# Differences of the blocks of x in the second phase: GpSimd in place of VectorE

## The chip, the cores and the metric

The kernel runs on one core of one Trainium2 chip. The metric is the device time of one execution in microseconds (us), from outside; three executions of the kernel before gave 1159.93, 1160.05 and 1161.06 us, median 1160.05. The engines in the profile are PE (TensorE matmuls), PEld (its weight loads), DVE (VectorE), ACT (ScalarE), POOL (GpSimd) and SP (SyncE, which issues all DMAs here).

## The reference

Linear attention over 8 batches and 8 heads, then a gated feed-forward layer on its output:

```python
def phi(x):
    proj = np.einsum('bhsd,df->bhsf', x, w_phi)
    proj = proj - np.max(np.abs(proj), axis=-1, keepdims=True)
    return np.concatenate([np.exp(proj), np.exp(-proj)], axis=-1)
q_p, k_p = (phi(q), phi(k))
kv = np.einsum('bhsf,bhsd->bhfd', k_p, v)
z = np.sum(k_p, axis=2)
num = np.einsum('bhsf,bhfd->bhsd', q_p, kv)
den = np.einsum('bhsf,bhf->bhs', q_p, z)[..., None] + 1e-06
attn = num / den                    # q, k, v: 8 x 8 x 576 x 64; w_phi: 64 x 128

x = attn.transpose(0, 2, 1, 3).reshape(4608, 512)
gate = 1.0 / (1.0 + np.exp(-(x @ w_gate)))      # 512 x 1536
val = x @ w_val                                 # 512 x 1536
out = gate * val @ w_out                        # 1536 x 512
```

## The kernel before

**Two phases.** The first phase (to about 610 us) makes the attention, writes its output x to DRAM in chunks of 512 tokens (`xscr`), and computes the part of the feed-forward layer that belongs to the first 512 of the 1536 hidden features (lines 914 and 971). The second phase does the other 1024 hidden features in two rounds of 512, each over 6 blocks of 768 tokens (`DC`): twelve passes of `pass_over`. Each pass adds its part of the output to what the rounds before left in DRAM.

**Precision by splitting.** A matmul in full float32 is replaced by three in the faster type float32r: each operand is split into a high part (a cast, on ScalarE) and a low part (the operand less its high part, a subtraction on VectorE), and high x high, high x low and low x high are summed.

**Blocks of x.** The products of the second phase are done on 2 x 2 blocks with seven products in place of eight, so that differences of the blocks of x are needed. `x_blocks` prepares them for one pass. It fetches four blocks of 128 x 768 (two of 128 features side by side, 384 tokens each) into `b11`, `tmp[0]` (block 12), `b22` and `b21`, makes four differences with `less` (the instruction is at line 1178), and splits seven blocks with `split`: a cast on ScalarE (line 1187) and a subtraction on VectorE (line 1191). The split of a fetched block is done in place: its low part overwrites the block, so it must wait until the differences that read the block are done. The differences are tmp[1] = tmp[0] - b11, tmp[2] = b22 - tmp[1], tmp[0] = b22 - tmp[0], and, once tmp[2] has been split, tmp[2] = b21 - tmp[2].

**A pass.** For each of two pairs of hidden blocks `group` runs seven products for the gate and seven for the value (line 1229: 6 matmuls of 128 x 384 each, into five PSUM banks named `bank`), and VectorE adds the products up (line 1242, one operand in PSUM, one in SBUF). `gated` applies the sigmoid on ScalarE, `valued` multiplies by the value (line 1280) and splits the result into its high (line 1284, ScalarE) and low part (line 1288, VectorE). Then six output tiles of 128 tokens are computed (line 1311: 12 matmuls of 128 x 512 each, 6 for each pair, into three PSUM banks named `gate`), and VectorE adds the earlier part from DRAM as it drains a bank (line 1139). The blocks of x of the next pass are fetched and made around the boundary between the products of one pass and its output tiles. In the first four passes VectorE also prepares weights for the second round (lines 796 to 867 and 1069 to 1094).

**What sets the order.** A planner (`Plan`) runs once on the host. Each step is given to it with an engine, a busy time, a lag, what it reads and writes and a rank; the planner simulates the engines, and from the steps that could start soonest takes the one with the lowest rank. The instructions are then written in the order of their planned starts. On the chip each engine works through its own queue in that order, and waits at an instruction until the semaphores of its inputs and of its output buffer are there.

Of the kernel before, what the change touches and what calls it, by code (L numbers as in the profile page):

```python
# [34 lines left out]
HT = 384  # L35
# [113 lines left out]
class Plan:  # L149


    SWITCH = 0.15
    NEAR = {"PE": 0.3, "DVE": 0.05, "ACT": 0.05, "SP": 0.0, "X": 0.0}
    SAME = {"PE": 0.0, "DVE": 0.12, "ACT": 0.13, "SP": 0.0, "X": 0.0}
    RATE = 0.26

    def __init__(self):
# [21 lines left out]
    def run(self):  # L179
        free = dict.fromkeys(self.NEAR, 0.0)  # L180
        ready = {e: [] for e in free}
# [31 lines left out]
        while left:  # L213
            best = None
            for e, cs in ready.items():
                ts = [(t, o) for o in cs if (t := start(o)) is not None]
                if not ts:
                    continue
                first = min(t for t, _ in ts) + self.NEAR[e]

# [32 lines left out]
            for n in o.then:  # L253
# [3 lines left out]
                else:  # L257
                    at = t + o.busy + self.SAME[o.eng]
                n.ready = max(n.ready, at)
# [8 lines left out]
def attention_moe(  # L268
# [9 lines left out]
    nc = tc.nc  # L278
    vec, act = nc.vector, nc.scalar
# [99 lines left out]
    plan = Plan()  # L379
# [4 lines left out]
    def dve(n, fn, reads, writes, rank, k=1.0, after=()):  # L384
        return plan.op("DVE", 0.07 + n / 960 / k, 0.16, fn, reads, writes, rank, after=after)

    def on_act(n, fn, reads, writes, rank, after=()):
        return plan.op("ACT", 0.08 + n / 1200, 0.17, fn, reads, writes, rank, after=after)

    def sp(size, fn, reads, writes, rank, after=()):  # L390
        return plan.op("SP", 0.06, size, fn, reads, writes, rank, after=after)
# [757 lines left out]
    def x_blocks(dc, r):  # L1149

        at_ = {n: (Buf([r_X], [P, 2, HT]), Buf([r_X], [P, 2, HT])) for n in XB}
        tmp = [Buf([r_tmp], [P, 2, HT]) for _ in range(3)]
        n_, since = [0.0], len(plan.ops)

        def rank():
            n_[0] += 0.1
            return r + n_[0]

        def fetch(x, K, h):
            t, e = dc * DC + h * HT, dc * DC + h * HT + HT  # L1160
            s = 0
            while t < e:
                c, o = divmod(t, CW)
                wd = min(CW - o, e - t)
                sp(
                    wd << 10,
                    lambda c=c, o=o, s=s, wd=wd: nc.sync.dma_start(
                        x().bitcast(F32)[:, :, s : s + wd],
                        xscr[c][:, 2 * K : 2 * K + 2, o : o + wd],
                    ),  # L1170
                    [xmark[c]], [x], rank(), prior[-1:],
                )
                t, s = t + wd, s + wd

        def less(o, a, b):
            dve(
                2 * HT,
                lambda: vec.tensor_tensor(  # L1178
                    o(), a().bitcast(F32), b().bitcast(F32), op=ALU.subtract
                ),  # L1180
                [x for x in (a, b) if x is not o], [o], rank(),
            )

        def split(n, src):
            xh, xl = at_[n]
            on_act(
                2 * HT, lambda: act.copy(xh(), src().bitcast(F32)), [src], [xh], rank()  # L1187
            )
            dve(
                2 * HT,  # L1190
                lambda: vec.tensor_tensor(
                    xl(), src().bitcast(F32), xh().bitcast(F32), op=ALU.subtract
                ),
                [src, xh] if src is not xl else [xh], [xl], rank(),
            )

        b11, b21, b22 = (at_[n][1] for n in ("11", "21", "22"))
        fetch(b11, 0, 0)
        fetch(tmp[0], 0, 1)
        fetch(b22, 1, 1)  # L1200
        fetch(b21, 1, 0)
        less(tmp[1], tmp[0], b11)
        split("11", b11)
        less(tmp[2], b22, tmp[1])
        split("T2", tmp[2])
        less(tmp[0], b22, tmp[0])
        split("T3", tmp[0])
        split("T1", tmp[1])
        less(tmp[2], b21, tmp[2])
        split("21", b21)  # L1210
        split("T4", tmp[2])
        split("22", b22)
        prior.append(plan.op("X", 0.0, 0.0, lambda: None, after=plan.ops[since:]))
        return at_
# [206 lines left out]
```

## Time and profile before

| what | us |
|---|---|
| median of three runs | 1160.05 |
| the profiled execution | 1160.85 |
| its span, first to last instruction | 1158.9 |
| TensorE busy | 1142.8 |
| VectorE busy | 933.3 |
| ScalarE busy | 583.0 |
| GpSimd busy (six instructions at the start) | 0.7 |

Times inside the program are counted from the start of the span. The profiled execution's own time is 1.95 us longer than its span. A line such as "L1178 DVE TENSOR_TENSOR more<-low,more x24" is a group: the line of the kernel, the engine, the operation, the tile written and the tiles read (`low`, `high`, `flat` and `more` are the four large SBUF areas in which the planner places its buffers, `bank` and `gate` are PSUM), and how often. In a timeline the two numbers ahead are the start and the length in us, and brackets behind name what ended the idle time in front of an instruction.

### The profile page before, as it was taken

What the parts mean: (1) busy time and instruction counts of PE and PEld (TensorE: products, weight loads), DVE (VectorE), ACT (ScalarE), POOL (GpSimd) and SP (SyncE); (2) the same over time, 40 slices, a digit from 0 to 9 for tenths busy, and PEclk for the clock granted to TensorE, in tenths of its full rate; (3) what the DMA queues carried; (4) which work ended last, traced back from release to release, by engine and by line L of the source; (5) the groups of instructions that cost most, each with busy time, mean ns of one, the idle gap of its engine ahead of it and who ended that gap; (6) DMA issues with size and microseconds to landing.
All of it is one profiled execution on the core that took longest, in us unless ns stands there. A gap on an engine that the chain in (4) does not pass through costs nothing.

```text
span 1158.9 us, 22323 instructions
## 1 busy us (share of the span) xinstructions
PE 1142.8 (99%) x8796; PEld 939.5 (81%) x8796; DVE 933.3 (81%) x1793; ACT 583.0 (50%) x1115; POOL 0.7 (0%) x6
## 2 busy tenths in 40 slices
PE   8999999999999999999999999999999999999998
PEld 6666566766676677678889999999999999999997
DVE  6999989888878878847897999988767757757764
ACT  6867776666656666635553444352332333323421
POOL 0000000000000000000000000000000000000000
PEclk9999999999999999999999999999999999999999
DMA  6764554344424443226526656545447433225122
GB/s 237 226 220 127 152 168 123 121 129 137 137 87 153 121 137 122 70 79 209 173 101 211 206 178 223 187 141 186 154 173 286 141 106 123 78 88 163 56 95 82
DMA packets 99441, 171.08 MB, mean 148 GB/s; under 512 B 18825, under 2 KB 43529, under 8 KB 99337
## 3 DMA queue, kind: packets, MB, share of 16 engines
q1 hardware_dynamic: 99336, 169.66, 45.7%
q8 instruction: 69, 1.13, 0.4%
q14 instruction: 36, 0.29, 0.1%
HBM read 120.06 MB, written 49.42 MB: 146 GB/s over the span
## 4 chain that ended last, share of the span: by engine, by line
PE 84%; DVE 7%; DMA 6%; ACT 2%; issue 1%; SPq 1%; DVEq 0%
PE bank L1229 30%; PE gate L1311 17%; PE gate L914 11%; PE gate L971 6%; PE bank L621 4%; PE bank L663 3%; PE bank L914 3%; DMA rb<-den 3%; PE bank L432 2%; PE bank L681 2%; DMA den<-dn 2%; PE bank L537 1%; DVE d L587 1%; PE bank L971 1%; PE bank L635 1%; PE bank L647 1%
## 5 line engine op out<-in xcount | busy, mean ns | idle before, releaser
L1229 PE MATMUL bank<-low,high 128*128 128x384 f32 x2016 | 351.8, 336 | 0.0
L1229 PEld LDWEIGHTS bank<-low,high 128*128 128x128 f32 x2016 | 349.8, 188 | 1.1
L1311 PE MATMUL gate<-low 128*128 128x512 f32 x864 | 198.4, 389 | 0.0
L1311 PEld LDWEIGHTS gate<-low 128*128 128x128 f32 x864 | 162.0, 188 | 33.2
L914 PE MATMUL gate<-low 128*128 128x512 f32 x696 | 165.7, 393 | 1.2 <-ACT flat L949 0.6
L914 PEld LDWEIGHTS gate<-low 128*128 128x128 f32 x696 | 128.6, 188 | 29.7 <-issue 1.2
L479 ACT ACTIVATE ek<-ek 128x512 f32<-128x512 f32 (+1 forms) x192 | 96.6, 526 | 27.3 <-DVE ek L467 25.9
L1242 DVE TENSOR_TENSOR more<-more,bank 128x384 f32<-128x384 f32 x111 | 61.1, 551 | 40.8 <-PE bank L1229 40.3
L971 PE MATMUL gate<-low 128*128 128x512 f32 x384 | 92.3, 394 | 0.0
L971 PEld LDWEIGHTS gate<-low 128*128 128x128 f32 x384 | 70.8, 188 | 15.1 <-issue 1.0
L621 PE MATMUL bank<-ek,vin 128*32 128x256 f32 x1240 | 74.5, 386 | 4.4 <-ACT d L545 3.8
L621 PEld LDWEIGHTS bank<-ek,vin 128*32 128x32 f32 x1240 | 37.8, 110 | 46.2 <-issue 11.0
L1139 DVE TENSOR_TENSOR flat<-gate,low 128x512 f32<-128x512 f32 x72 | 49.3, 685 | 23.3 <-PE gate L1311 11.7
L438 DVE TENSOR_REDUCE mk<-bank 128x4 f32<-128x512 f32 (+1 forms) x92 | 49.0, 552 | 21.3 <-PE bank L432 16.9
L1242 DVE TENSOR_TENSOR flat<-flat,bank 128x384 f32<-128x384 f32 x75 | 41.3, 551 | 29.3 <-PE bank L1229 29.1
L1187 ACT CAST low<-more 128x768 fp32r<-128x768 f32 x36 | 30.1, 836 | 61.1 <-DVE more L1178 60.8
L467 DVE TENSOR_TENSOR ek<-bank,mk 128x512 f32<-128x512 f32 (+1 forms) x92 | 48.2, 550 | 0.6 <-ACT d L550 0.2
L1267 ACT ACTIVATE more<-more 128x384 f32<-128x384 f32 x38 | 20.0, 525 | 57.1 <-DVE more L1242 56.9
L938 ACT CAST low<-flat 128x512 fp32r<-128x512 f32 x36 | 22.3, 620 | 51.5 <-DVE flat L963 44.9
L1284 ACT CAST low<-more 128x384 fp32r<-128x384 f32 x50 | 24.7, 513 | 46.6 <-DVE more L1280 46.6
L590 ACT ACTIVATE eq<-d 128x1152 f32<-128x1152 f32 x29 | 33.9, 1168 | 24.8 <-DVE d L587 24.4
L432 PE MATMUL bank<-wk,kin 64*128 64x128 f32 x496 | 38.7, 289 | 4.6 <-DMA kin<-k 4.3
(184 smaller groups left out, 1700.1 us busy)
## 6 DMA issues: line engine op xcount, KB each, us to landing
flat<-w_moe SPq DMA_DIRECT2D x36, 512.0 KB
low<-xs SPq DMA_DIRECT2D x46, 256.0 KB
kin<-k SPq DMA_DIRECT2D x32, 320.0 KB
qin<-q SPq DMA_DIRECT2D x32, 320.0 KB
vin<-v SPq DMA_DIRECT2D x32, 320.0 KB
ys<-flat SPq DMA_DIRECT2D x36, 256.0 KB
low<-ys SPq DMA_DIRECT2D x36, 256.0 KB
yt<-flat SPq DMA_DIRECT2D x36, 256.0 KB
```

Of the source, the lines that this page charges most:

```text
L432: nc.tensor.matmul(pk[hd]()[:, t, :], x()[head(hd), t * P : t * P + P], wk[head(hd), :], start=True, stop=True,)
L438: vec.tensor_reduce(mx, pk, axis=AX.X, op=ALU.max, apply_absolute_value=True)
L467: vec.tensor_tensor(ek[g]()[:, :, F:], src, mk[g]()[:, :ns].unsqueeze(2).broadcast_to([P, ns, F]), op=ALU.subtract,)
L479: lambda g=g, sg=sg: act.activation(ek[g]()[:, :, sg * F : sg * F + F], ek[g]()[:, :, F:], AF.Exp, scale=1.0 - 2.0 * sg,),
L621: nc.tensor.matmul(o_[o : o + Q, : 2 * F], vx()[:, 2 * t + hd, o % D : o % D + Q], (e0, e1)[hd][:, t, :] if t < 4 else e2[:, 0, :], start= ...
L663: nc.tensor.matmul(nm()[o : o + Q, :], w()[:, sg, o : o + Q], es[sg]()[:, o // D, cs], start=sg == 0, stop=sg == 1, tile_position=(0, o),)
L914: nc.tensor.matmul(o(), a()[:, ws], x(), start=cc + n == 0, stop=cc == NC4 - 1 and n == 2,)
L971: nc.tensor.matmul(acc(), a()[:, ts], w(), start=first and i == 0, stop=last and i == 2)
L1139: lambda: vec.tensor_tensor(y(), acc(), y1().bitcast(F32), op=ALU.add),
L1229: nc.tensor.matmul(o()[:, :HT], s()[:, ws], y()[:, cc, :], start=first and cc + i_ == 0, stop=cc + i_ == 3, skip_group_check=not first,)
L1242: lambda: vec.tensor_tensor(o(), p(), q()[:, :HT], op=ALU.add),
L1311: nc.tensor.matmul(acc(), s()[:, h, o : o + P], w(), start=i + e + k_ == 0, stop=i + e + k_ == 4,)
```

## The change

The subtraction in `less` is issued on GpSimd in place of VectorE. The planner gets GpSimd as a further engine, with a busy time of 2.0 and a lag of 0.2 for each difference, and plans all engines anew.

```diff
-    NEAR = {"PE": 0.3, "DVE": 0.05, "ACT": 0.05, "SP": 0.0, "X": 0.0}
-    SAME = {"PE": 0.0, "DVE": 0.12, "ACT": 0.13, "SP": 0.0, "X": 0.0}
+    NEAR = {"PE": 0.3, "DVE": 0.05, "ACT": 0.05, "SP": 0.0, "POOL": 0.0, "X": 0.0}
+    SAME = {"PE": 0.0, "DVE": 0.12, "ACT": 0.13, "SP": 0.0, "POOL": 0.15, "X": 0.0}
...
         def less(o, a, b):
-            dve(
-                2 * HT,
-                lambda: vec.tensor_tensor(
+            plan.op(
+                "POOL", 2.0, 0.2,
+                lambda: nc.gpsimd.tensor_tensor(
                     o(), a().bitcast(F32), b().bitcast(F32), op=ALU.subtract
                 ),
                 [x for x in (a, b) if x is not o], [o], rank(),
```

What the planner makes of it is seen at two places. The first is the boundary of the ninth pass, at about 1002 us of the profile before. VectorE's queue before, from the add of the last product on; names in brackets are the semaphores of engines and DMA queues that a row waits for:

```order
L1242 TENSOR_TENSOR more<-more,bank_182 128x384 [waits PE_49]
L1288 TENSOR_TENSOR low<-flat,low 128x384 [waits Activation_49]
L1288 TENSOR_TENSOR low<-more,low 128x384 [waits Activation_49]
L1280 TENSOR_TENSOR flat<-flat,more 128x384 [waits DVE_49]
L1178 TENSOR_TENSOR flat<-more,low 128x768 [waits DMAHW4_49,DMAHW1_49]
L1288 TENSOR_TENSOR low<-flat,low 128x384 [waits Activation_49]
L1191 TENSOR_TENSOR low<-low 128x768 [waits DVE_49]
L1139 TENSOR_TENSOR flat<-gate_213,low 128x512 [waits DMAHW5_49,DMAHW3_49,PE_49]
L1178 TENSOR_TENSOR more<-low,flat 128x768 [waits DMAHW2_49]
```

The same place of VectorE's queue now, from the multiplication (L1280) that stands two rows ahead of that add:

```order
L1280 TENSOR_TENSOR more<-more 128x384 [waits DVE_49]
L1242 TENSOR_TENSOR flat<-flat,bank_182 128x384 [waits PE_49]
L1288 TENSOR_TENSOR low<-more,low 128x384 [waits Activation_49] x2
L1280 TENSOR_TENSOR flat<-flat 128x384 [waits DVE_49]
L1191 TENSOR_TENSOR low<-low 128x768 [waits DMAHW4_49,DMAHW1_49,Pool_49]
L1288 TENSOR_TENSOR low<-flat,low 128x384 [waits Activation_49]
L1191 TENSOR_TENSOR low<-more,low 128x768 [waits Activation_49]
L1139 TENSOR_TENSOR flat<-gate_213,low 128x512 [waits DMAHW5_49,PE_49]
L1191 TENSOR_TENSOR low<-more,low 128x768 [waits Activation_49]
```

The differences (L1178) are gone from the queue, and the split of block 11 (the first L1191) waits for GpSimd. They stand on GpSimd's queue alone, here the four of this boundary and the first of the next one:

```order
L1178 TENSOR_TENSOR more<-flat,low 128x768 [waits DMAHW1_49,DMAHW4_49,DMAHW0_49,DVE_49]
L1178 TENSOR_TENSOR more<-low,more 128x768 [waits DMAHW2_49,DVE_49,Pool_49]
L1178 TENSOR_TENSOR flat<-low,flat 128x768
L1178 TENSOR_TENSOR more<-low,more 128x768 [waits DMAHW5_49,DMAHW3_49,DVE_49]
L1178 TENSOR_TENSOR flat<-more,low 128x768 [waits DMAHW4_49,DMAHW7_49,DMAHW2_49,DVE_49]
```

The first waits for its DMAs and for a buffer that VectorE frees, the second for the first and its own block, the third for nothing more, the fourth for its block and for VectorE, which splits the second.

The second place is TensorE's queue at the start of the second phase, at about 599 us, as a difference of the two orders:

```order
 L1229 MATMUL bank_192<-low,high 128x384 x6
+L1229 MATMUL bank_182<-low,high 128x384 x6
 L971 MATMUL gate_213<-low 128x512 x12
 L971 MATMUL gate_206<-low 128x512 x12
 L971 MATMUL gate_219<-low 128x512 x12
-L971 MATMUL bank_182<-low 128x512 x12
-L1229 MATMUL bank_180<-low,high 128x384 x6
+L971 MATMUL bank_180<-low 128x512 x12
```

The second product of the first pass has moved ahead of the 48 matmuls of L971 that end the first phase. VectorE's queue there now:

```order
L935 TENSOR_TENSOR flat<-flat,bank_194 128x512 [waits PE_49,Activation_49]
L1069 TENSOR_TENSOR flat<-high 128x512 [waits DVE_49]
L1191 TENSOR_TENSOR low<-more,low 128x768 [waits Activation_49]
L940 TENSOR_TENSOR low<-flat,low 128x512 [waits Activation_49]
L1083 TENSOR_TENSOR flat<-flat 128x256 [waits DVE_49]
L1191 TENSOR_TENSOR low<-flat,low 128x768 [waits Pool_49]
L1242 TENSOR_TENSOR more<-more,bank_182 128x384 [waits PE_49]
```

The first L1191 makes the low operand of that second product, and the L1242 drains it.

## The prediction

> **What bounds the kernel now.** I read the engines' busy time first, then the chain that ended last, then the stretches around the change.
>
> ```profile
> span 1158.9 us, 22323 instructions
> PE 1142.8 (99%) x8796; PEld 939.5 (81%) x8796; DVE 933.3 (81%) x1793; ACT 583.0 (50%) x1115; POOL 0.7 (0%) x6
> ```
>
> TensorE is the bound: 16.1 us of the span are not its own. VectorE has the second highest load, GpSimd is empty. Where are the 16.1 us? These are the last pieces of the chain, in order of time (start, length, what):
>
> ```profile
> 610.46 28.08 PE bank L1229 x162
> 638.54 16.36 PE gate L1311 x72
> ...
> 956.94 16.36 PE gate L1311 x72
> 973.29 29.12 PE bank L1229 x168
> 1002.42 16.36 PE gate L1311 x72
> 1018.77 29.12 PE bank L1229 x168
> ```
>
> Each piece starts where the one before ends: in the second phase the chain is TensorE alone, 45.48 us a pass (29.12 of L1229, 16.36 of L1311). Busy time by stretch (us, then PE, weight loads, DVE, ACT, POOL) says the same for a pass in which VectorE also makes weights, for a later one, and for one boundary of two passes:
>
> ```profile
> 655.00:700.00 45.00, 45.00 (x240) 42.20 (x239) 44.47 (x86) 20.90 (x39) 0.00 (x0) 1.00 0.65 215
> 1019.00:1064.00 45.00, 45.00 (x239) 42.20 (x238) 31.29 (x53) 15.02 (x27) 0.00 (x0) 1.00 0.32 99
> 1002.00:1019.00 17.00, 17.00 (x78) 14.16 (x77) 15.86 (x24) 6.60 (x10) 0.00 (x0) 1.00 0.48 134
> ```
>
> TensorE is full in all three at full granted clock. So VectorE time given back here buys nothing by itself. But VectorE is close behind: 44.47 of 45 us in an early pass, 15.86 of 17 at the boundary. That boundary is where the changed instructions stand, so the question is the margin there.
>
> **The margin at a boundary.** VectorE at the end of the pass that ends at 1002.42, in order of time:
>
> ```profile
> 1001.59 0.55 DVE L1242 TENSOR_TENSOR more<-more,bank 128x384 f32<-128x384 f32 x1
> 1002.17 0.56 DVE L1280 TENSOR_TENSOR more<-more 128x384 f32<-128x384 f32 x1
> 1002.65 0.55 DVE L1242 TENSOR_TENSOR more<-more,bank 128x384 f32<-128x384 f32 x1
> 1003.11 0.55 DVE L1288 TENSOR_TENSOR low<-flat,low 128x384 fp32r<-128x384 f32 x1
> 1004.03 0.56 DVE L1288 TENSOR_TENSOR low<-more,low 128x384 fp32r<-128x384 f32 x1 [0.37 <-ACT low L1284]
> 1004.51 0.55 DVE L1280 TENSOR_TENSOR flat<-flat,more 128x384 f32<-128x384 f32 x1
> 1004.98 0.95 DVE L1178 TENSOR_TENSOR flat<-more,low 128x768 f32<-128x768 f32 x1
> ```
>
> The L1288 of 1004.03 makes the last low part that the second half of the first output tile needs. TensorE starts that half two groups of six after the boundary; 72 matmuls take 16.36 us, so a group takes 1.36 and it is due at 1002.42 + 2.73 = 1005.15. This L1288 ends at 1004.59. The margin is 0.56 us. (Four of the twelve output stages have this order, two tiles first, and five have it in the new order; the others put three first and have 1.36 us more.) ScalarE shows when the inputs of the differences land:
>
> ```profile
> 1001.54 0.84 ACT L1187 CAST low<-low 128x768 fp32r<-128x768 f32 x1 [0.46 <-DMA low<-xs]
> 1002.75 0.84 ACT L1187 CAST low<-low 128x768 fp32r<-128x768 f32 x1
> 1003.91 0.83 ACT L1187 CAST low<-low 128x768 fp32r<-128x768 f32 x1
> ```
>
> Block 11 arrives at 1001.54; the next two casts did not wait for their DMA, so those blocks are there by 1002.75 and 1003.91. On VectorE the first difference stood behind the L1288 rows, at 1004.98. On a free GpSimd queue it will start at about 1001.55, in the middle of them.
>
> **The change part by part.** Removed from VectorE: the differences.
>
> ```profile
> L1178 DVE TENSOR_TENSOR more<-low,more x24: 944/950/954, 599.8 to 1103.9; 128x768 f32<-128x768 f32 x24
> L1178 DVE TENSOR_TENSOR flat<-more,low x8: 948/950/960, 641.3 to 1005.0; 128x768 f32<-128x768 f32 x8
> ```
>
> With the other 16, 48 x 0.950 = 45.6 us, four in each of twelve sets of blocks. Since TensorE waits for nothing there, the gain is 0. No DMA is issued by these steps; some fetches of L1167 into the temporaries come a few rows earlier in SP's queue, at a DMA share of 0.32 to 0.65, which I count as 0.
>
> Added to GpSimd: 48 instructions of 128x768 with two inputs. The nearest rows:
>
> ```profile
> masks.py:199 POOL TENSOR_SCALAR_AFFINE_SELECT ident<-ident 128x128 f32<-128x128 f32 x1 | 0.3, 295 | 0.1
> masks.py:197 POOL MEMSET ident<- 128x128 f32 x1 | 0.2, 205 | 0.3 <-POOLq L1371 0.3
> L1371 POOL MEMSET const-float32-0.0<- 128x1 f32 x1 | 0.1, 99 | 0.2 <-issue 0.2
> ```
>
> A memset of one element takes 99 ns, of 128 takes 205, so 0.83 ns an element: 0.1 + 768 x 0.83 = 0.74 us is the lower end. The select has one input and 295 ns, 1.54 ns an element: 1.28 us. Twice that slope, for two inputs, gives 2.47 us, the upper end. I take six times the select, 1.77, say 1.8 us: between one input and two. [...]
>
> New waits. The in-place split of block 11 (L1191) now waits for GpSimd on VectorE's queue, and one or two L1288, all L1139 drains of the output and the next pass's L1242 are queued behind it; so do the splits of the two blocks that later differences read. ScalarE's casts of the differences wait for GpSimd in place of VectorE. TensorE waits for L1288 and L1139. If GpSimd runs undisturbed: 1001.55 + 3 x 1.8 gives 1003.35, 1005.15 and 1006.95 for the first three, earlier than the 1004.98 and later at which VectorE started them. These waits cost 0 as long as a difference stays under about 2.4 us; beyond, at the two boundaries where the first drain stands behind the split that waits for the third difference, that drain, due before the seventh group (1002.42 + 6 x 1.36 = 1010.6), falls behind.
>
> One term is there in any case, at the first set. TensorE's second product of the first pass now stands ahead of 48 matmuls of L971, where before it came after them.
>
> ```profile
> 587.62 10.88 PE bank L914 x48
> 598.50 1.04 PE bank L1229 x6
> 599.54 8.20 PE gate L971 x36
> ```
>
> Its low operand is made by an L1191 that stands on VectorE's queue behind an L935, which needs the last L914 (598.50), and an L1069. The prices of the three:
>
> ```profile
> 597.65 0.68 DVE L1069 TENSOR_TENSOR flat<-high 128x512 f32<-128x512 f32 x1
> ...
> 598.86 0.68 DVE L935 TENSOR_TENSOR flat<-flat,bank 128x512 f32<-128x512 f32 x1
> 601.86 0.95 DVE L1191 TENSOR_TENSOR low<-more,low 128x768 fp32r<-128x768 f32 x1
> ```
>
> L935 from 598.6, and, each starting 0.6 us behind the one before as in these rows, L1069 from 599.2, L1191 from 599.8 to 600.75. The second matmul of the product wants it at 599.7: 1.05 us late, between 0 and 2.
>
> **The unknown: both engines on SBUF together.** Differences and L1280, L1288, L1191 all read two operands from SBUF. GpSimd has 0.7 us of work in the whole trace, so no row shows the two side by side. One end: no effect, 0. The other: they take turns, a whole instruction at a time. Worked out for the rows above by the new order, with 1.8 us: first difference 1001.55 to 1003.35; the L1280 of 1002.17 moves to 1003.35 and ends at 1003.90; L1242 reads PSUM and runs at 1003.8; the second difference has taken its turn at 1003.90 and holds until 1005.70; then the two L1288. If VectorE, being back to back, keeps its turn, the second L1288 ends at 5.70 + 0.47 + 0.55 = 1006.7, 1.55 us late. If the third difference gets in between, it ends at 5.70 + 0.55 + 1.80 + 0.55 = 1008.6, 3.45 late. Mean 2.5 us. With 0.74 us a difference the worse order ends at 1005.4, 0.3 late; with 2.47 it ends at 1010.6, 5.4 late. There are eleven boundaries with a next set of blocks: 11 x 2.5 = 27.5, with ends of 0 and 59.
>
> I take the turns: even a much weaker interference than a full turn beats a margin of 0.56 us, and in the early passes VectorE has 0.53 us left in 45, while each set trades 3.8 us of its own time for up to four turns of up to 1.8. [...]
>
> **Sum.** The profiled execution took 1160.85 (span 1158.9 and 1.95 around it). 1160.85 + 0 + 1.05 + 27.5 = 1189.4; the median of the runs lies 0.8 below the profiled one: 1188.6, say 1189.
>
> **Rivals.**
> - *No effect between the engines; not slower.* GpSimd hides the differences wholly. For it: TensorE's chain has no gap, and the chain of differences would even end earlier than now. Against it: the margin. Time: 1160.05 + 1.05 = 1161.1, within 0.2% of before (about what a measurement of this kernel can tell from no change). It decides if VectorE's L1280 and L1288 stay at 0.55 us beside GpSimd.
> - *A weaker interference.* VectorE's instructions pass first or both only stretch. If each of the three two-input rows above loses half its length, 0.28, the lateness is 0.84 - 0.56 = 0.28 us; if one whole turn falls on them, up to 1.2 less what the margin takes, about 0.9 with the drains behind. 11 times that is 3 to 10: 1164 to 1171.
> - *GpSimd itself is slow.* At 3 us without any turns the third difference ends at 1001.55 + 9 = 1010.55, the split of 0.95 and the drain of 0.6 behind it 1.5 us after they are due, at two boundaries: 3 us, 1164. I count it with the weaker interference.
> - *Faster.* Only if the freed 45.6 us met a wait of TensorE; the chain shows none behind 610. At most the noise of the runs.
> That the change does nothing is no rival: all 48 instructions stand on GpSimd's queue.
>
> **How the numbers follow.** Turns 0.60 (own range 1172 to 1203: 1.0 to 3.8 us a boundary), weaker interference or a slow GpSimd 0.14, no effect 0.23, faster 0.03. So slower 0.74, same 0.23, faster 0.03. The time is 1189; the range reaches down to the no-effect case and up to 1201, where about 0.1 of the first case lies beyond.
>
> **What would show it.** Right: L1288 and L1280 rows at a boundary with 1 to 2 us instead of 0.55, L1178 on GpSimd near 1.8 us or stretched, TensorE waiting in L1311 for L1288 or L1139, 2 to 3 us in each boundary, passes of 47 to 49 us. Wrong: those rows at 0.55 us, a chain of L1229 and L1311 with no gap, passes of 45.48 us; then only VectorE's sum falls, by 45.6. In the first pass a wait of L1229 at about 599.7 of 1 us shows the other term.

## The result and the profile after

The changed kernel took 1207.67 us (median of four runs, 1205.74 to 1208.81), the kernel before beside it 1160.03: a ratio of 1.0405, 95% interval 1.0388 to 1.0422. It is slower by 47.6 us where 29 were forecast. The profiled execution took 1205.74. The head of its page:

```profile
span 1204.0 us, 22413 instructions
PE 1161.7 (96%) x8796; PEld 944.4 (78%) x8796; DVE 959.8 (80%) x1745; ACT 582.5 (48%) x1115; POOL 98.9 (8%) x54
```

VectorE has 48 instructions fewer and is busy for 26.5 us more. The 45.6 us of differences are gone, so the rest of its work has become 72 us longer. Which rows? The lines L1280, L1288 and L1242 by form (shortest, median and longest duration in ns, then the first and last start):

```profile
L1280 DVE TENSOR_TENSOR flat<-flat,more x25: 546/553/2247, 642.7 to 1184.5; 128x384 f32<-128x384 f32 x25
L1280 DVE TENSOR_TENSOR more<-more,bank x12: 542/546/549, 627.5 to 1181.9; 128x384 f32<-128x384 f32 x12
L1288 DVE TENSOR_TENSOR low<-more,low x52: 543/556/2292, 628.2 to 1183.5; 128x384 fp32r<-128x384 f32 x52
L1242 DVE TENSOR_TENSOR more<-more,bank x106: 540/553/555, 606.1 to 1180.9; 128x384 f32<-128x384 f32 x106
```

Rows with two operands in SBUF reach 2.2 to 2.3 us. Rows of the same size and even the same line with one operand in PSUM (`bank`) never exceed 0.56. The differences on GpSimd:

```profile
L1178 POOL TENSOR_TENSOR more<-flat,low x7: 1871/1886/1909, 579.0 to 1135.0; 128x768 f32<-128x768 f32 x7
L1178 POOL TENSOR_TENSOR more<-low,more x24: 1851/2073/2527, 591.4 to 1145.8; 128x768 f32<-128x768 f32 x24
```

1.85 to 1.89 us where the row waits for nothing, about 2.1 where it waits for VectorE. The boundary of the ninth pass, now at 1037.84, in order of time, first VectorE, then GpSimd:

```profile
1038.63 4.11 DVE L1288 TENSOR_TENSOR low<-more,low 128x384 fp32r<-128x384 f32 x2
1042.66 2.19 DVE L1280 TENSOR_TENSOR flat<-flat 128x384 f32<-128x384 f32 x1
...
1049.12 2.24 DVE L1191 TENSOR_TENSOR low<-low 128x768 fp32r<-128x768 f32 x1
```

```profile
1038.30 1.89 POOL L1178 TENSOR_TENSOR more<-flat,low 128x768 f32<-128x768 f32 x1 [37.70 <-DVE more L1280]
1040.26 2.06 POOL L1178 TENSOR_TENSOR more<-low,more 128x768 f32<-128x768 f32 x1
1042.29 2.15 POOL L1178 TENSOR_TENSOR flat<-low,flat 128x768 f32<-128x768 f32 x1
1048.68 1.87 POOL L1178 TENSOR_TENSOR more<-low,more 128x768 f32<-128x768 f32 x1 [4.24 <-DVE low L1191]
```

The engines alternate, one whole instruction each: difference to 1040.19, L1288, difference to 1042.32, L1288, difference to 1044.44, L1280. VectorE never gets two turns in a row, although its queue is full; wherever differences stand back to back in this trace, at most one two-operand row gets through between two of them. What TensorE makes of it:

```profile
1037.84 4.05 PE L1311 MATMUL gate<-low 128*128 128x512 f32 x17
1042.80 4.64 PE L1311 MATMUL gate<-low 128*128 128x512 f32 x19 [0.91 <-DVE low L1288]
1047.79 5.74 PE L1311 MATMUL gate<-low 128*128 128x512 f32 x24 [0.35 <-DVE flat L1139]
1054.62 3.01 PE L1311 MATMUL gate<-low 128*128 128x512 f32 x12 [1.09 <-DVE flat L1139]
```

The chain without a gap is broken three times: once for the low part, twice for output drains, the last of which stand behind the L1191 that met the fourth difference. TensorE's waits over the whole program (line, what it waited for: us, times, longest):

```profile
PE gate L1311 <- DVE low L1288: 12.5, 12, 1.8
PE gate L1311 <- DVE flat L1139: 4.9, 9, 1.1
PE gate L1311 <- ACT low L1284: 4.4, 5, 1.0
...
PE bank L1229 <- DVE low L1191: 3.0, 1, 3.0
...
PE bank L1229 <- ACT low L1187: 1.0, 1, 1.0
```

This list counts idle time by modelled ends. Measured from start to start of the matmuls (a gap less the 0.227 us of a matmul of L1311), the same waits are 14.5 for L1288, 6.3 for L1139 and 5.5 for L1284. The next section uses one measure for all kernels, worked out from these starts: the length of each stage less its length before (16.36 us for 72 matmuls of L1311, 29.12 for 168 of L1229). "Start" is the stage that holds the first products and the last of L971, less the 40.04 us that it took before. The stages are those of the profiled execution, which took between 3.7 us less (write_only, 1160.51) and 3.5 us more (fourth, 1168.21) than the median beside it.

| kernel | start | eleven boundaries (L1311) | other stages | median, us | ratio, 95% interval |
|---|---|---|---|---|---|
| changed kernel | 6.7 | 38.8 | 0.8 | 1207.7 | 1.0388 to 1.0422 |
| order_dve | 5.2 | 16.9 | 0.6 | 1183.3 | 1.0172 to 1.0218 |
| old_order | 1.9 | 17.2 | 1.2 | 1185.7 | 1.0184 to 1.0244 |
| write_only | 2.0 | 0.0 | 0.4 | 1164.3 | 1.002 to 1.004 |
| beside_read | 1.6 | 18.7 | 3.1 | 1182.2 | 1.0164 to 1.0205 |
| beside_write | 0 | 7.2 | 1.2 | 1169.0 | 1.0047 to 1.0094 |
| first_set | 0 | 40.4 | 0.4 | 1200.6 | 1.0327 to 1.0362 |
| fourth | 0 | 1.3 | 4.3 | 1164.7 | 1.0024 to 1.0054 |
| halves | 6.1 | 29.1 | 0.8 | 1196.8 | 1.0299 to 1.033 |
| after_lows | 8.1 | 12.7 | 9.7 | 1190.7 | 1.0232 to 1.028 |
| late_gated | 0.6 | 0.2 | 6.8 | 1168.8 | 1.0042 to 1.0072 |
| late_gated_16 | 0.4 | 0.2 | 5.2 | 1166.4 | 1.0049 to 1.0074 |
| shift_only | 0.6 | 0.2 | 6.5 | 1167.0 | 1.0052 to 1.0076 |

In the changed kernel ten boundaries lose 3.0 to 5.1 us each, and the sixth loses 0: there block 22 lands late, and the differences start 2.5 us before the boundary and 6 us after it, beside nothing that TensorE waits for.

### The profile page after: what moved, and what is told of

Same layout as the page of the kernel before. It is cut to its first block, busy times and chain, and to the rows that moved or that the text cites. A ratio compares the mean times of both kernels' runs of the same rounds, so it can differ in the third digit from the quotient of the medians.

```text
span 1204.0 us, 22413 instructions
## 1 busy us (share of the span) xinstructions
PE 1161.7 (96%) x8796; PEld 944.4 (78%) x8796; DVE 959.8 (80%) x1745; ACT 582.5 (48%) x1115; POOL 98.9 (8%) x54
## 4 chain that ended last, share of the span: by engine, by line
PE 70%; DVE 19%; DMA 5%; issue 4%; ACT 3%; SPq 1%; DVEq 0%; ACTq 0%
PE bank L1229 24%; PE gate L914 11%; PE gate L1311 8%; PE gate L971 6%; PE bank L621 4%; PE bank L663 3%; DVE low L1191 3%; PE bank L432 2%; DVE low L1288 2%; PE bank L914 2%; PE bank L681 2%; DVE flat L1280 2%; DMA rb<-den 2%; DMA low<-xs 1%; PE bank L537 1%
## 5 line engine op out<-in xcount | busy, mean ns | idle before, releaser
L1229 PE MATMUL bank<-low,high 128*128 128x384 f32 x2016 | 353.6, 337 | 4.2 <-DVE low L1191 3.0
L1229 PEld LDWEIGHTS bank<-low,high 128*128 128x128 f32 x2016 | 350.3, 188 | 6.5 <-DVE low L1191 3.2
L1311 PE MATMUL gate<-low 128*128 128x512 f32 x864 | 215.1, 405 | 22.1 <-DVE low L1288 12.5
L1311 PEld LDWEIGHTS gate<-low 128*128 128x128 f32 x864 | 165.5, 194 | 68.5 <-DVE low L1288 18.6
L914 PE MATMUL gate<-low 128*128 128x512 f32 x696 | 165.7, 394 | 1.2 <-ACT flat L949 0.6
L914 PEld LDWEIGHTS gate<-low 128*128 128x128 f32 x696 | 128.6, 188 | 29.7 <-issue 1.2
L479 ACT ACTIVATE ek<-ek 128x512 f32<-128x512 f32 (+1 forms) x192 | 96.7, 526 | 29.1 <-DVE ek L467 27.8
L1242 DVE TENSOR_TENSOR more<-more,bank 128x384 f32<-128x384 f32 x106 | 58.4, 551 | 48.5 <-PE bank L1229 48.1
L971 PE MATMUL gate<-low 128*128 128x512 f32 x384 | 93.7, 399 | 0.0
L971 PEld LDWEIGHTS gate<-low 128*128 128x128 f32 x384 | 72.0, 191 | 15.5 <-issue 1.0
L1178 POOL TENSOR_TENSOR more<-flat,low 128x768 f32<-128x768 f32 x7 | 13.2, 1887 | 796.6 <-DMA ys<-flat 577.7
L1139 DVE TENSOR_TENSOR flat<-gate,low 128x512 f32<-128x512 f32 x72 | 48.8, 683 | 34.5 <-DMA out<-flat 24.0
L1242 DVE TENSOR_TENSOR flat<-flat,bank 128x384 f32<-128x384 f32 x76 | 41.8, 551 | 30.3 <-PE bank L1229 29.8
L1178 POOL TENSOR_TENSOR more<-low,more 128x768 f32<-128x768 f32 x24 | 51.2, 2133 | 69.9 <-DVE low L1191 59.0
L1284 ACT CAST low<-more 128x384 fp32r<-128x384 f32 x52 | 25.8, 513 | 60.6 <-DVE more L1280 60.6
L1284 ACT CAST low<-flat 128x384 fp32r<-128x384 f32 x44 | 22.1, 513 | 53.7 <-DVE flat L1280 53.7
```

The costliest lines, as they stand in the source:

```text
L479: lambda g=g, sg=sg: act.activation(ek[g]()[:, :, sg * F : sg * F + F], ek[g]()[:, :, F:], AF.Exp, scale=1.0 - 2.0 * sg,),
L914: nc.tensor.matmul(o(), a()[:, ws], x(), start=cc + n == 0, stop=cc == NC4 - 1 and n == 2,)
L971: nc.tensor.matmul(acc(), a()[:, ts], w(), start=first and i == 0, stop=last and i == 2)
L1139: lambda: vec.tensor_tensor(y(), acc(), y1().bitcast(F32), op=ALU.add),
L1178: lambda: nc.gpsimd.tensor_tensor(o(), a().bitcast(F32), b().bitcast(F32), op=ALU.subtract),
L1229: nc.tensor.matmul(o()[:, :HT], s()[:, ws], y()[:, cc, :], start=first and cc + i_ == 0, stop=cc + i_ == 3, skip_group_check=not first,)
```

## Experiments

**The new order without GpSimd (order_dve).** The plan of the changed kernel, the instruction back on VectorE:

```diff
-                lambda: nc.gpsimd.tensor_tensor(
+                lambda: vec.tensor_tensor(
```

> The new order of all queues, with the differences issued on VectorE at the places that the planner gave them. Theory A (GpSimd and VectorE instructions that read two operands from SBUF take turns): no turns, so most of the 47 us goes: 1160 to 1170, the rest being the first product of T2 and differences of 0.95 us that now stand ahead of some L1288. Theory B (the new order itself costs the time): about 1207. Theory C (what costs is waiting for GpSimd's results, which take twice as long): as A, 1160 to 1170.

1183.26 us, and neither expectation met it. No row is stretched (L1288 has a mean of 553 and 554 ns in its two forms, L1280 548 to 554). TensorE waits for the drains instead:

```profile
PE gate L1311 <- DVE flat L1139: 10.4, 10, 2.2
PE bank L1229 <- DVE low L1191: 3.3, 1, 3.3
```

The plan gives VectorE the 3.8 us of four differences less per set; put back into that order they come ahead of drains, which then end after TensorE needs their banks.

**The old order with GpSimd (old_order).** The plan of before, the instruction on GpSimd:

```diff
-                lambda: vec.tensor_tensor(
+                lambda: nc.gpsimd.tensor_tensor(
```

> The order planned for VectorE, with the differences issued on GpSimd. Theory A: the differences still start when their blocks land, beside L1280 and L1288, so 1185 to 1210. Theory B: 1160 to 1162. Theory C: VectorE's splits wait at other places of its queue; 1160 to 1180, with L1280 and L1288 at 0.55 us.

1185.70 us. L1288 now has a mean of 740 and 779 ns in its two forms (554 before), and TensorE waits for it:

```profile
PE gate L1311 <- DVE low L1288: 8.6, 8, 2.5
```

So the meeting of the engines costs 25 us in an order that was not made for it. Together with the 23 of order_dve this makes 48, nearly the whole, but the next run shows that it is no sum of two causes.

**The new order, GpSimd as long but hardly reading (write_only).** Each difference is left out but for four elements a partition; two memsets fill the time:

```diff
-                lambda: nc.gpsimd.tensor_tensor(
-                    o(), a().bitcast(F32), b().bitcast(F32), op=ALU.subtract
-                ),
+                lambda: [
+                    nc.gpsimd.tensor_tensor(
+                        o()[:, :, :: HT - 1], a()[:, :, :: HT - 1].bitcast(F32),
+                        b()[:, :, :: HT - 1].bitcast(F32), op=ALU.subtract,
+                    ),
+                    nc.gpsimd.memset(o()[:, :, 1 : HT - 1], 0.0),
+                    nc.gpsimd.memset(o()[:, :, 1 : HT - 1], 0.0),
+                ],
```

> The changed kernel with its queues unaltered, but each of the 48 differences is left out on GpSimd: four elements a partition are subtracted (so that the waits for both blocks stay), and the rest of the output tile is written twice over with memsets of 128x764, which read nothing. About 1.9 us of GpSimd a difference, as in the changed kernel. Theory A (GpSimd's reading of SBUF beside VectorE's two-operand instructions is the cause; the new order does no harm once VectorE has the 3.8 us a set to spare): L1280 and L1288 stay near 0.55 us, the eleven boundaries lose under 0.5 us each, the start 1 to 2 us; 1160 to 1168. Theory B (GpSimd's length and the new order, splits ahead of low parts and drains, are the cause whatever GpSimd does meanwhile): boundaries lose 1.5 to 4 us as before; 1180 to 1207.

1164.25 us, as theory A had it. GpSimd is busy for 91.1 us instead of 98.9. VectorE's L1288 (L1293 in this kernel) is back at its length, and TensorE's one wait in the second phase is that of the start:

```profile
L1293 DVE TENSOR_TENSOR low<-more,low 128x384 fp32r<-128x384 f32 x52 | 28.5, 554 | 5.7 <-ACT low L1289 4.1
L1183 POOL MEMSET more<- 128x764 f32 x36 | 27.0, 751 | 2.1
PE bank L1234 <- DVE low L1196: 1.7, 1, 1.7
```

All eleven boundaries lose 0.0. The queues are those of the changed kernel and GpSimd takes 1.9 us a difference, so at the boundaries neither the order nor GpSimd's length costs anything by itself; at the start 2.0 us are left. What the run takes away is the reading of 128x768 from SBUF, and with it go 44.5 of the 47.6 us (47.6 less the 3.1 that this kernel has over before). No run reads without writing, so whether reading alone would do the same is not shown.

**Useless reads, useless writes (beside_read, beside_write).** To the kernel before, behind four casts of each set, are added two GpSimd subtractions of 128x384 each (reading the cast), or six memsets of a spare tile:

```diff
             act.copy(xh(), src().bitcast(F32))
+            if n in ("11", "21", "22", "T4"):
+                for h in range(2):
+                    x = xh()[:, h, :].bitcast(F32)
+                    nc.gpsimd.tensor_tensor(stage["spare"], x, x, op=ALU.subtract)
```

> The kernel before, and on GpSimd four pairs of subtractions of 128x384 for each set of blocks, which read the casts of blocks 11, 21, 22 and T4 twice and write a spare tile that nobody reads; about 1 us each. Theory A: turns of 1 us on L1280, L1288 and L1191, with VectorE's own 0.95 us differences on top: 1175 to 1205, VectorE's two-operand rows at up to 1.6 us. Theories B and C: nothing waits for these instructions, 1160 to 1161.

```diff
             act.copy(xh(), src().bitcast(F32))
+            if n in ("11", "21", "22", "T4"):
+                act.copy(stage["dot"], stage["spare"][:, :1])
+                for _ in range(6):
+                    nc.gpsimd.memset(stage["spare"], 0.0)
```

> The kernel before, and on GpSimd at the same places six memsets of 128x384 for each of the four blocks, about 2 us together, each set started by a ScalarE copy of one column. They read nothing from SBUF. Theory A in the form that the shared thing is reading: 1160 to 1163 (ScalarE's 48 small copies), VectorE's rows at 0.55 us. Theory A in the form that any GpSimd instruction on SBUF keeps VectorE out: 1175 to 1205.

1182.20 us, within theory A's range, and 1169.02 us, between the two ranges that were expected. VectorE's L1288 (L1296, L1298) and L1280 with a PSUM operand (L1288, L1290), first with the reads, then with the writes (after the bar: busy us, mean ns):

```profile
L1296 DVE TENSOR_TENSOR low<-flat,low 128x384 fp32r<-128x384 f32 x46 | 33.8, 737 | 3.4 <-ACT low L1292 3.3
L1288 DVE TENSOR_TENSOR more<-more,bank 128x384 f32<-128x384 f32 x12 | 6.6, 547 | 0.0
```

```profile
L1298 DVE TENSOR_TENSOR low<-flat,low 128x384 fp32r<-128x384 f32 x46 | 25.5, 554 | 15.6 <-ACT low L1294 15.4
L1290 DVE TENSOR_TENSOR more<-more,bank 128x384 f32<-128x384 f32 x12 | 6.6, 547 | 0.0
```

The reads slow VectorE with nothing depending on them (737 ns in the form shown, where the kernel before has 554); the writes leave it untouched (554). The 8.5 us that beside_write still lost in the second phase are put down to its own trigger, a ScalarE copy that waits for the memsets ahead (27.0 us in 21 waits; VectorE's idle time in front of L1298 that ScalarE ended is 15.4 us, above, and 2.2 in the kernel before). No run takes the trigger away alone; write_only has none and loses nothing at the boundaries.

**Parts of the change (first_set, fourth, halves).** The first of the twelve sets keeps its differences on VectorE; only the fourth difference of each set goes to GpSimd; each difference is made as two instructions of 128x384 (the two conditions below belong to two kernels; the names behind # are added here):

```diff
+            if len(prior) == 1:                        # first_set
+            if o is not tmp[2] or b is not tmp[2]:     # fourth
+                dve(
+                    2 * HT,
+                    lambda: vec.tensor_tensor(
...
+                return
```

```diff
+                lambda: [                              # halves
+                    nc.gpsimd.tensor_tensor(
+                        o()[:, h, :], a()[:, h, :].bitcast(F32),
+                        b()[:, h, :].bitcast(F32), op=ALU.subtract,
+                    )
+                    for h in range(2)
+                ],
```

> As the change, but the first set of blocks (the start of the second phase) keeps its differences on VectorE. Theory A with the loss at the start put down to turns and a half clock: the 5.6 us there go, 1201 to 1203. Rival (the start is late for another reason, or the loss only moves): 1206 to 1208.

1200.61 us: 7 less than the changed kernel, just under the range of theory A. The start term is 0, so it is made by the first set alone.

> Only the fourth difference of each set on GpSimd, the first three on VectorE. Theory A: it starts behind the split of T2, when L1280 and L1288 are through, so 1160 to 1165. If any difference on GpSimd costs its quarter: 1172.

1164.69 us. L1288 stays at 554 ns; the fourth difference meets only splits, and waits for its own turns (mean 2963 ns). The 4.3 us of the other stages are not explained.

> As the change, each difference as two GpSimd instructions of 128x384. Theory A with strict alternation, one VectorE instruction for each GpSimd one: a turn lasts about 1 us in place of 2, the first L1288 rows are late by about 0.9 us in place of 2.2, fewer half clocks: 1178 to 1190. Theory C (the length of GpSimd's chain counts, which is the same or longer): 1205 to 1215.

1196.82 us: the direction was right, the size not. Shorter turns are also more of them, and at 1.00 us undisturbed (median 1.35) two halves are longer than a whole:

```profile
L1179 POOL TENSOR_TENSOR more<-low,more x48: 1000/1346/1751, 591.5 to 1137.1; 128x384 f32<-128x384 f32 x48
```

**The differences held back (after_lows, late_gated).** A GpSimd copy of one element of the last L1288 output of the pass that ends is put ahead of the next set, so that the differences start behind the rows at the boundary; late_gated does so for the last six sets alone and leaves the first six on VectorE (the line with # is in late_gated only, and the remark is added here):

```diff
+            held.append(plan.op(
+                "POOL", 0.15, 0.1,
+                lambda: nc.gpsimd.tensor_copy(dot, hl()[:, 1, :1].bitcast(F32)),
+                [(hl, 1)], [], rank(),
+            ))
...
+            if len(prior) < 7:                         # late_gated: VectorE, as before
...
-                [x for x in (a, b) if x is not o], [o], rank(),
+                [x for x in (a, b) if x is not o], [o], rank(), after=held[-1:],
```

> As the change, but a GpSimd copy of one column of the last low part (L1288) of a pass stands ahead of the next set's differences, so that these start about 4 us later, behind L1280 and L1288. Theory A: L1280 and L1288 at 0.55 us, turns only on L1191, and the drains L1139 some 0 to 1 us late: 1160 to 1175. Theory C: the chain from block to split ends 4 us later, 1207 or more.

1190.66 us, between the two expectations: no boundary from the fifth on loses more than 0.15 us, but the start (8.1), the first three boundaries (8.4, 2.3, 1.8) and the products that stand between the output tiles of the fourth (1.4, counted under other stages) do. There VectorE has hardly anything free (44.47 of 45 us busy before), and the held-back differences delay its splits and drains instead: TensorE waits 9.6 us for L1139 (L1140 in this kernel), in four waits. Part of the 9.7 us of the other stages has another cause, which the next run brought out.

> The first six sets of blocks take their differences on VectorE as before the change; the last six on GpSimd, held back by a one-element GpSimd copy of the last low part (L1288) of the pass that is ending, so that they start behind the rows that TensorE waits for. Theory A (only the meeting of two-operand reads with the low parts at the boundary costs time, and in the late passes VectorE has room for the rest): no start term, early boundaries 0, late ones 0 to 0.5: 1160 to 1165. Theory B (GpSimd's reads cost VectorE time wherever they stand): at least 1.5 us for each of the six late sets, 1169 or more.

1168.81 us: theory B's time, but not its mechanism. The boundaries lose 0.2 us in all, as theory A has it. About 0.55 us is lost in each product stage instead, in those of the early passes without a GpSimd instruction too, and without a gap. The matmuls of L1229 follow each other after 176.7 ns in these two kernels and after 173.3 in all the others. Both have a new 4-byte scratch tile that lies ahead of the four areas in SBUF.

**The scratch tile (late_gated_16, shift_only).** The tile made 64 bytes a partition; and the kernel before with the 4-byte tile alone:

```diff
-    dot = const.tile([P, 1], F32, name="dot")
+    dot = const.tile([P, 16], F32, name="dot")
```

```diff
     wk = const.tile([P, F], F32, name="wk")
+    dot = const.tile([P, 1], F32, name="dot")
+    nc.gpsimd.memset(dot, 0.0)
```

> As in the kernel that takes the last six sets on GpSimd behind a gate, but the scratch tile of the gate is 64 bytes a partition instead of 4. In both gated kernels every matmul of the products followed the one before after 176.7 ns, in all others after 173.3, in every pass, those without a GpSimd instruction included. Theory A (the 4-byte tile moved the areas behind it in SBUF, and that alone slows the matmuls' reading; 64 bytes keep the alignment): 173.3 ns again, 2016 x 3.34 ns = 6.7 us less than the 1168.8 of the former, so 1161 to 1164. Theory B (the gate or the late differences cost the time): 176.7 ns and 1167 to 1170 as before.

> The kernel before with nothing but a scratch tile of 4 bytes a partition added ahead of the four SBUF areas (and one memset of it at the start). Theory A (the place of the areas slows the matmuls): 176.7 ns from matmul to matmul in L1229, 1160.4 + 6.7, so 1166 to 1169. Theory B (it does not): 173.3 ns, 1160 to 1162.

1166.35 and 1166.95 us. The tile alone brings the kernel before to 176.7 ns a matmul and to the time that was expected. 64 bytes don't undo it (176.1 ns), so the range for late_gated_16 was missed. The products' group in before, shift_only and late_gated_16 (busy us, mean ns of one):

```profile
L1229 PE MATMUL bank<-low,high 128*128 128x384 f32 x2016 | 351.8, 336 | 0.0
```

```profile
L1231 PE MATMUL bank<-low,high 128*128 128x384 f32 x2016 | 358.7, 339 | 0.1
```

```profile
L1246 PE MATMUL bank<-low,high 128*128 128x384 f32 x2016 | 357.3, 338 | 0.0
```

Without the 5.6 us that its slower product matmuls cost (0.4 and 5.2 in the table), late_gated_16 would be at 1160.8, 0.1% above the 1159.56 of before beside it: gated differences on GpSimd cost next to nothing in the late passes, and gain nothing. No version beat the kernel before.

## Why the prediction was right and wrong

- *The bound and the sign: right.* The freed 45.6 us of VectorE bought nothing, and TensorE's chain lost time where the differences meet two-operand rows.
- *GpSimd's 1.8 us: right* (1.85 to 1.89).
- *The turns: right, and always in the worse of the two orders.* That the engines take turns at all was an assumption, as the trace before has no row of one beside the other; the rows above show it, with L1288 and L1280 at up to 2.29 and 2.25 us in place of 0.55. The prediction took the mean of both orders; the rows above alternate strictly.
- *The margin of 0.56 us: wrong.* It was reckoned to the group of six. TensorE waits in front of the single matmul that reads the low part, the 18th of the stage: x17 stands ahead of its first wait in the rows above (the 24th where three tiles stand first, as at the first boundary). Due was 1002.42 + 17 x 0.227 = 1006.28, the margin 1.7. The worse order's 3.45 less those 1.14 gives 2.3 us; measured are 14.5 + 5.5 = 20.0 us for L1288 and L1284 in ten boundaries, 2.0 each. That the term of 2.5 comes near is luck: two errors nearly cancelled in it.
- *The step that failed: a boundary was priced by that one lateness alone.* Three costs behind it are missing from the 27.5: the drains L1139 behind the splits that meet later differences, the fourth among them (6.3 us; the prediction put these waits at 0 with GpSimd undisturbed and added nothing for them in the case of turns), the half clock after a wait (7.7: in five boundaries matmuls of L1311 follow each other after 0.427 us in place of 0.227), and small gaps and restarts (the remaining 4.8). 20.0 + 6.3 + 7.7 + 4.8 = 38.8. The lateness itself came to 20.0 and not 27.5, which hid 7.5 of these 18.8.
- *The start, 1.05 us: mis-sized by six times.* Undisturbed it is 2.0 (write_only). In the changed kernel it is 6.7:

```profile
599.32 0.44 PE L1229 MATMUL bank<-low,high 128*128 128x384 f32 x1 [0.97 <-ACT low L1187]
602.72 1.97 PE L1229 MATMUL bank<-low,high 128*128 128x384 f32 x5 [2.95 <-DVE low L1191]
604.48 9.84 PE L971 MATMUL gate<-low 128*128 128x512 f32 x36
```

```profile
600.51 0.68 DVE L935 TENSOR_TENSOR flat<-flat,bank 128x512 f32<-128x512 f32 x1
601.11 0.68 DVE L1069 TENSOR_TENSOR flat<-high 128x512 f32<-128x512 f32 x1
601.72 0.95 DVE L1191 TENSOR_TENSOR low<-more,low 128x768 fp32r<-128x768 f32 x1
```

The wait of 1 us that the prediction named is there, but for the high operand; the low one costs 2.95 more. The three rows on VectorE follow each other as worked out, but the first starts at 600.51 instead of 598.6, behind weight rows that the working left out. Some of these had met the first differences: L851 took 2.24 us at 591.83, and 0.69 at the same place of write_only's queue, where the L935 starts 0.9 us after the first product and not 3.4. Then 36 matmuls of L971 take 9.84 us instead of 8.20, the first 3.1 us of them at half clock.

- *The rivals.* "No effect" and "a weaker interference" are out: the rows reach 2.2 us, a full turn.

The second phase lost 6.7 + 38.8 + 0.8 = 46.3 us; it began 1.2 us sooner (first product at 597.1, before at 598.3). That leaves 45.1, and the two spans differ by 1204.0 - 1158.9 = 45.1.

## What to carry to other kernels

Work given to an idle GpSimd was not free here when it read SBUF: a difference of 1.9 to 2.5 us could hold up a VectorE instruction with two SBUF operands for a whole turn (L1288 took up to 2.29 us in place of 0.55; in write_only, with hardly any reading, 0.55). So count the turns that fall on rows that the critical engine waits for, assume the worse order, and let GpSimd do such work only where those rows are not. When a wait is priced, find the single instruction that waits, then add what stands behind it: the next buffers to be drained and the clock of the engine that was kept waiting (0.427 us a matmul of L1311 in place of 0.227 here). When an experiment adds a tile, compare a stage that it should not touch: 4 bytes a partition ahead of the large areas cost 3.3 ns a product matmul here (shift_only).

## What the runs showed that was not expected

**Half clock after a short lull.** In the changed kernel TensorE ran at half clock in six pieces of the second phase (3.41 us each, the first 6.83; none in that phase before, up to its last output tiles). They start at 600.8, 652.0, 703.2, 802.2, 945.5 and 996.7, all whole multiples of 3.413 us apart (996.7 - 600.8 is 116 of them). Windows on that grid (us; then busy time and count of PE, weight loads, DVE, ACT, POOL; granted clock, DMA share and GB/s):

```profile
648.55:651.96 3.41, 1.07 (x5) 0.30 (x3) 3.41 (x5) 1.74 (x4) 2.00 (x1) 1.00 0.00 0
652.00:655.40 3.40, 3.40 (x8) 2.75 (x9) 3.40 (x6) 2.18 (x3) 0.00 (x0) 0.50 0.00 0
...
750.98:754.40 3.42, 1.79 (x8) 1.50 (x9) 3.42 (x6) 2.28 (x4) 0.22 (x1) 1.00 0.01 2
...
993.30:996.70 3.40, 1.90 (x7) 1.01 (x8) 3.40 (x7) 2.45 (x4) 0.00 (x0) 1.00 0.00 0
```

The window ahead of each piece holds 5 to 7 matmuls where a full one holds 15 of L1311. A pause as long (1.77 us ahead of 752.61) that was shared by two windows, with 15 and 8 matmuls, brought none. The five boundaries with a piece lost 4.5 us on average, the five others that lost time 3.3. TensorE was not idle in these windows: half clock followed 1.07 to 1.90 us of matmuls. Among this trace's windows at full clock the count of matmuls tells them apart (7 in the last row, 8 in the row ahead) and the modelled busy time does not, but that is no rule: in halves two windows of 8 matmuls and 1.61 us each, from 652.18 and from 699.97, end differently, and only the second is followed by half clock. What decides is open.

**A row with one operand.** The TENSOR_SCALAR of L843, with one 128x512 uint32 operand in SBUF, was held up too: its longest row takes 2.08 us, at 579.13 beside a difference that runs from 579.05 to 580.93, where the median is 0.42 and no row of the kernel before takes over 0.44. So the rows to count are not only those with two SBUF operands.

**The place of a tile.** 4 bytes a partition ahead of the large areas cost every product matmul 3.3 ns, 2016 x 3.34 = 6.7 us in all, and 64 bytes 2.7 ns. Which address property decides was not tried.
